# A fused chunked-attention and feed-forward kernel: how block 0's rows are loaded, and where block 2's turns stand

## The chip, the cores and the metric

The kernel runs on 1 core of one Trainium2 chip. The metric is the device time of one execution in microseconds (us), here the median of several runs. The engines are PE (TensorE; PEld are its weight loads), DVE (VectorE), ACT (ScalarE), POOL (GpSimd) and SP (SyncE). DMAs are issued from the queues of SP, ACT and Pool.

## The reference

Attention over q, k, v of shape (4 batches, 8 heads, 768 positions, 64), in chunks of 32 positions. A chunk sees 16 positions before it, itself, 8 after it, and 8 memory rows of its head (mem_k, mem_v):

```
for c in range(24):
    q_c  = q[:, :, 32*c : 32*c+32]
    ctx  = slice(max(0, 32*c-16), min(768, 32*c+40))
    k_full, v_full = concat(mem_k, k[ctx]), concat(mem_v, v[ctx])
    a = softmax(q_c @ k_full.T / 8)
    out[:, :, chunk c] = a @ v_full
x = out with heads side by side, (3072 tokens, 512)
y = (relu(x @ w_gate) * (x @ w_val)) @ w_out      # 512 -> 1536 -> 512
```

Inputs and the result are float32; the kernel computes in float16 with float32 sums in PSUM.

## The kernel before

The 3072 tokens are cut into 8 blocks of 384 (two per batch). A block's attention works on pairs of heads (hp 0 to 3). Its feed-forward part has twelve **units** of 128 hidden columns, `ffn_unit` (four g_ps matmuls, whatever stands in `between`, four v_ps matmuls, then a relu on ACT and a product gv on DVE, L323 to L351), and three output units `out_unit` (L353) with twelve o_ps matmuls each. The attention of block n + 1 is laid between the units of block n. The order of all instructions is written out by hand (`manual_schedule`), and each engine works its own list in order.

**Layout of queries and keys.** The matmuls need them turned, with the 64 dimensions on partitions. For blocks 0 to 2 the rows come in as they lie in memory (four positions a row: `k_rows`, `q_rows`, and two rows of memory keys by `load_rows_mem`) into the float16 tiles `rk` and `rq`; `turn_pe` (L177) turns them by 16 matmuls for a head pair against a selection matrix and an identity, and `turn_copy` (L196) copies the result from PSUM to SBUF on DVE, one copy for block 0 and two for blocks 1 and 2. Block 2's turn takes the PSUM tile that scores use as well (tag "sc", one buffer). From block 3 on the DMA engines turn (`turn_dma`) and Pool spreads the queries (`spread_q`).

**Block 0's rows.** A DMA from Pool's queue casts float32 to float16 on its way. SP's and ACT's don't: they bring float32 into the staging tiles `kst` and `qst`, and a copy on DVE or ACT casts it into `rk` and `rq` (`cast`, L445). Before the change heads 0 to 3 go by staging (the loop of L384: SP brings keys, ACT queries, two heads a DMA), heads 4 to 7 by Pool (L436 to L438). Pool's list then has the values of block 0 (`load_band`, four DMAs), the memory keys for the later blocks (`fetch_mem(memk, mem_k)`, L441), and the weights `load_w` in pieces of 256 columns, two DMAs each (L442, L443, L497, L498, L514, L515), with block 1's and block 2's rows and values between them. SP spreads the memory values over the value tile (`load_mem_v`, four small DMAs).

**Block 0's attention** (L461 to L508): `step_s0` (mask and score matmuls, exponential on ACT), `wide_d` (sums by matmul, then logarithm on ACT), `wide_e` (reciprocal by an exponential on ACT), `wide_v` (values by matmul, then the product xT on DVE), for each head pair. `fill` issues matmuls on a zero tile at the start. The first feed-forward matmuls of block 0 are in `chunk` (L456).

**Blocks 2 to 7** (`run`, L585): the units are gone through in order; `at` gives for each head pair the unit after which its scores are computed. Values (`step_v`) come two units later inside a unit, the product (`step_m`) three units later. For block 2, at = (2, 5, 8, 11), and a pair's turn stands one unit before its scores, behind that unit. `clear` holds six sets of DVE memsets, one behind each of the units 0 to 5.

Of the kernel before, what the change touches and what calls it, by code (L numbers as in the profile page):

```python
# [8 lines left out]
F32 = mybir.dt.float32  # L9
# [8 lines left out]
def kernel(  # L18
# [58 lines left out]

    ident = const.tile([128, 128], F16, name="ident")
    sels = [const.tile([128, NQ, 32], F16, name=f"sel{p}") for p in range(2)]
    kst = const.tile([KR + 2, H // 2, J * D], F32, name="kst")  # L80
    qst = const.tile([QR, H // 2, J * D], F32, name="qst")
    k16s = [const.tile([128, NQ, H, D], F16, name=f"k16{p}") for p in range(2)]

    vwins = [const.tile([128, NQ, H, 2 * D], F16, name=f"vwin{p}") for p in range(2)]
# [29 lines left out]
    def rows_of(n):  # L114
        if n not in rows:
            rows[n] = (half.tile([KR + 2, H, J * D], F16, tag="rk", name="rk"),
                       half.tile([QR, H, J * D], F16, tag="q16", name="rq"))
        return rows[n]

    def load_rows_mem(dma, dst, n, h0, nh):  # L120
        src = bass.AP(tensor=mem_k.tensor, offset=mem_k[n // 2, h0, 0, 0].offset,
                      ap=[[J * D, 2], [NMEM * D, nh], [1, J * D]])
        dma(dst, src)

    def load_rows(n, h0, nh):
        rk, rq = rows_of(n)
        pool_dma(rk[0:KR, h0:h0 + nh], k_rows(n, h0, nh))
        pool_dma(rq[:, h0:h0 + nh], q_rows(n, h0, nh))
# [9 lines left out]
    def fetch_mem(dst, src_t):  # L138
        pool_dma(dst, bass.AP(tensor=src_t.tensor, offset=src_t[0, 0, 0, 0].offset,
                              ap=[[D, NMEM], [NMEM * D, B * H], [1, D]]))  # L140
# [36 lines left out]
    def turn_pe(n, hp):  # L177

        if n != 1:
            pool, tag = (pools["t"], "t") if n == 0 else (sps, "sc")  # L180
            ps = pool.tile([128, 2, 512], F32, tag=tag, name="kq_ps")
            kps, qps = ps[:, 0], ps[:, 1, 0:TB]
        else:
            ps, kps, qps = None, bank("k_ps"), bank("q_ps")[:, 0:TB]
        turns[n, hp] = ps, kps, qps
        rk, rq = (t.rearrange("p h (j d) -> p h j d", j=J) for t in rows_of(n))
        sel = sels[n % 2].rearrange("p i t -> p (i t)")

        for t, dst, w in ((rk, kps, sel[0:KR + 2]), (rq, qps, ident[:QR, :QR])):
            steps = dst.rearrange("p (r j) -> p j r", j=J) if n == 0 else dst.rearrange("p (j r) -> p j r", j=J)  # L190
            for j in range(J):
                for hh in range(2):
                    nc.tensor.matmul(steps[D * hh:D * hh + D, j], lhsT=t[:, 2 * hp + hh, j], rhs=w,
                                     start=True, stop=True)

    def turn_copy(n, hp):  # L196
        if n not in kTs:
            kq = turned.tile([128, HP, 512 + TB], F16, tag="kq", name="kq")
            kTs[n] = kq[:, :, 0:512].rearrange("p a (i m) -> p i a m", i=NQ)
            qTs[n] = kq[:, :, 512:].rearrange("p a (i m) -> p i a m", i=NQ)  # L200
            turns[n] = kq
        ps, kps, qps = turns.pop((n, hp))
        if n == 0:
            dve_copy(turns[n][:, hp], ps.rearrange("p a c -> p (a c)")[:, 0:512 + TB])
        else:
            for src, dst in ((kps, turns[n][:, hp, 0:512]), (qps, turns[n][:, hp, 512:])):
                dve_copy(dst.rearrange("p (r j) -> p r j", j=J), src.rearrange("p (j r) -> p r j", j=J))  # L207
# [28 lines left out]
    def step_s0(n, hp):  # L236

        sc = sps.tile([128, 2, 512], F32, tag="sc", name="sc_ps")
        mq = bass.AP(tensor=maskq.tensor, offset=maskq.offset, ap=[maskq.ap[0], [0, NQ], [1, QB]])
        for hh in range(2):  # L240
            nc.tensor.matmul(sc[:, hh, 0:TB].rearrange("p (i m) -> p i m", m=QB), lhsT=maskk, rhs=mq,
                             start=True, stop=False)
        score_mms(n, hp, sc, False)
        ex = epool.tile([128, 2, NQ, QB], F16, tag="ex", name="ex")
        nc.scalar.activation(ex.rearrange("p h i m -> p h (i m)"), sc[:, :, 0:TB], ACT.Exp, scale=SCALE)
        exs[n, hp] = ex
# [25 lines left out]
    def wide_d(n, hp):  # L272
        ex = exs[n, hp]
        for i0, i1, kind in ((0, 1, 1), (1, NQ, 0)) if n == 0 else ((0, NQ - 1, 0), (NQ - 1, NQ, 2)):
            for hh in range(2):
                nc.tensor.matmul(xs[D * hh:D * hh + D, QB * i0:QB * i1], lhsT=ones[:, kind, :],
                                 rhs=ex[:, hh, i0:i1, :], start=True, stop=True)
        nc.scalar.activation(xs, xs, ACT.Ln, scale=1.0 / 64.0)

    def wide_e(n, hp):  # L280
        rinv = rpool.tile([128, TB], F32, tag="rw", bufs=4, name="rw")
        nc.scalar.activation(rinv, xs, ACT.Exp, scale=-1.0, bias=mln64)
        rinvs[n, hp] = rinv

    def wide_v(n, hp):
        ex = exs.pop((n, hp))
        for i in range(NQ):
            for hh in range(2):
                nc.tensor.matmul(xo[D * hh:D * hh + D, QB * i:QB * i + QB], lhsT=vwins[n][:, i, 2 * hp + hh, 0:D],
                                 rhs=ex[:, hh, i, :], start=True, stop=True)  # L290
        nc.vector.tensor_tensor(out=x_of(n)[:, hp, :], in0=xo, in1=rinvs.pop((n, hp)), op=ALU.mult)
# [87 lines left out]
    def fill(count):  # L379
        for i in range(count):  # L380
            nc.tensor.matmul(xo, lhsT=filler[:, 0:128], rhs=filler[:, 0:TB], start=True, stop=True)


    for hp in range(HP // 2):  # L384
        sp(kst[0:KR, 2 * hp:2 * hp + 2], k_rows(0, 2 * hp, 2))
        act_dma(qst[:, 2 * hp:2 * hp + 2], q_rows(0, 2 * hp, 2))
        if hp == 0:
            load_rows_mem(sp, kst[KR:KR + 2], 0, 0, H // 2)
    nc.scalar.preload_act_table_set("natural_log_exp_and_others")

    def words(t):
# [41 lines left out]
    select(ident, 1.0, 0, [[-1, 128]], 1)  # L433
    build_sel(0)
    fetch_mem(memv, mem_v)
    load_rows(0, 4, 2)  # L436
    load_rows_mem(pool_dma, rows_of(0)[0][KR:KR + 2, H // 2:H], 0, H // 2, H // 2)
    load_rows(0, 6, 2)  # L438
    load_band(0, v, vwins)
    load_mem_v(0)  # L440
    fetch_mem(memk, mem_k)  # L441
    load_w(0, 256)  # L442
    load_w(256, 512)  # L443

    def cast(t, hp, eng):  # L445
        dst, src, n = rows_of(0)[t], (kst, qst)[t], (KR + 2, QR)[t]
        eng(dst[0:n, 2 * hp:2 * hp + 2], src[:, 2 * hp:2 * hp + 2])
# [11 lines left out]
                ffn_mm(n, x, f, a)  # L459

    with tc.tile_pool(name="tps", bufs=2, space=bass.MemoryType.PSUM) as pools["t"]:  # L461
        fill(12)
        cast(0, 0, dve_copy)
        for t, hp in ((1, 0), (1, 1), (0, 1)):
            cast(t, hp, act_copy)
        turn_pe(0, 0)
        turn_copy(0, 0)
        fill(4)
        step_s0(0, 0)
        turn_pe(0, 1)  # L470
        turn_copy(0, 1)
        wide_d(0, 0)
        wide_e(0, 0)
        step_s0(0, 1)
        turn_pe(0, 2)
        turn_copy(0, 2)
        wide_d(0, 1)
        wide_e(0, 1)
        turn_pe(0, 3)
        turn_copy(0, 3)  # L480
    pools["f"] = ctx.enter_context(tc.tile_pool(name="fps", bufs=4, space=bass.MemoryType.PSUM))
    step_s0(0, 2)
    wide_v(0, 0)
    wide_d(0, 2)
    step_s0(0, 3)
    wide_e(0, 2)


# [6 lines left out]
    select(bias, 0.0, -NMEM, [[0, 3]], 1, ALU.is_ge)  # L495
    select(bias, NEG, NMEM + 55, [[32, 3]], -1, ALU.is_ge)
    load_w(512, 768)  # L497
    load_w(768, 1024)  # L498

    ffn_open(0, (0, 1))  # L500
# [78 lines left out]
    def pieces(n, what):  # L579
        for w, hp in what:  # L580
            STEP[w](n, hp)
# [3 lines left out]
    def run(order, n, at, turn_at):  # L585
        for u, (b, x) in enumerate(order):
            now = [hp for hp in range(HP) if n < NB and u == at[hp] + 2]
            if n < NB:
                pieces(n, [("m", hp) for hp in range(HP) if u == at[hp] + 3])
            inner, outer = ("ve", "") if x >= NDC else ("v", "e")  # L590
            unit(b, x, [lambda w=(w, hp): pieces(n, [w]) for hp in now for w in inner])
            pieces(n, [(w, hp) for hp in now for w in outer])
            if n < NB:
                pieces(n, [("s", hp) for hp in range(HP) if u == at[hp]])
            if n == 2:
                for hp in range(HP):
                    if u == at[hp] - 1:
                        turn_pe(n, hp)
                        turn_copy(n, hp)
                if u < len(clear):  # L600
                    clear[u]()
            if u == turn_at and n + 1 < NB:
                turn_dma(n + 1)
                spread_q(n + 1)
# [44 lines left out]
```

## Time and profile before

| what | value |
|---|---|
| median of 7 runs | 241.52 us (240.37 to 242.7) |
| the profiled execution | 240.37 us, span 238.5 us |
| PE busy | 227.0 us, 95% of the span |
| ACT busy | 142.2 us, 60% |
| DVE busy | 105.5 us, 44% |
| POOL busy | 101.5 us, 43% |
| packets of Pool's queue (q0), share of 16 engines over the span | 80.4% |
| packets of SP's (q1) and ACT's queue (q10) | 19.9%, 8.5% |

A share of busy time is a mean over stages that have different limits, so it has to be read by stretches of time. Columns named "idle before" give the time that an engine stood still before an instruction, and after "<-" what ended it. Packets overlap in the DMA engines, so their summed share can be over 100%. The bytes of a casting DMA are counted as they are written, at half of what is read.

### The profile page before, as it was taken

Reading aid. Unit: us, or ns where it says so; the run is one execution under the profiler, and the core shown is the slowest. Engines: PE = TensorE matmul, PEld = TensorE weight load, DVE = VectorE, ACT = ScalarE, POOL = GpSimd, SP = SyncE. Lnnn points to the kernel's source line nnn. Section 1 sums busy time; section 2 is a strip of 40 time slices with the busy share of each in tenths; the row PEclk is TensorE's granted clock in tenths of the full one; section 3 lists DMA queues with packets and bytes.
Section 4 is the critical chain, followed back from the end, with each engine's and each line's share of the span. In section 5 each row is a group of like instructions: output and inputs, shape, how many; then the busy total and the mean of one; then the engine's idle time right before and its main releaser. Section 6 shows DMA issues by size and latency. Waiting matters only on the chain.

```text
span 238.5 us, 4610 instructions
## 1 busy us (share of the span) xinstructions
PE 227.0 (95%) x1736; PEld 131.0 (55%) x1736; DVE 105.5 (44%) x208; ACT 142.2 (60%) x300; POOL 101.5 (43%) x129
## 2 busy tenths in 40 slices
PE   7869799999999999999999999999999999999993
PEld 3635454555544566546664666556664666456541
DVE  3545647878611055612662146505551266313400
ACT  3663494377752388827984489628892698434321
POOL 8998665935219901990069503980130000000000
PEclk9999999999999999999999999999999999999998
DMA  7999999999997999599929997999902100120012
GB/s 164 137 165 194 193 179 195 174 192 148 127 160 119 193 168 132 35 166 129 175 28 111 195 143 80 65 186 138 137 0 83 49 3 0 47 88 0 1 44 88
DMA packets 107831, 27.61 MB, mean 116 GB/s; under 512 B 91730, under 2 KB 104866, under 8 KB 107810
## 3 DMA queue, kind: packets, MB, share of 16 engines
q0 software_dynamic: 82560, 15.16, 80.4%
q1 hardware_dynamic: 21378, 5.61, 19.9%
q10 hardware_dynamic: 3872, 6.56, 8.5%
q8 instruction: 13, 0.21, 0.3%
q14 instruction: 8, 0.07, 0.1%
HBM read 31.13 MB, written 6.29 MB: 157 GB/s over the span
## 4 chain that ended last, share of the span: by engine, by line
PE 75%; DMA 12%; POOL 5%; DVE 4%; ACT 2%; issue 2%; POOLq 0%; DVEq 0%
PE o_ps L360 25%; PE g_ps L334 22%; PE v_ps L334 21%; DMA wv<-in_moe_w_val_dram 11%; PE sc_ps L258 3%; DVE kq L207 2%; PE xo_ps L298 2%; PE xs_ps L298 2%; POOL vwin L136 2%; DVE gv L341 1%; DMA out_dram<-o_sb 1%; ACT ln L302 1%; POOL wg L166 1%; ACT gr L340 1%; PE sc_ps L233 1%
## 5 line engine op out<-in xcount | busy, mean ns | idle before, releaser
L341 DVE TENSOR_TENSOR gv<-v_ps,gr 128x384 f16<-128x384 f32 x95 | 52.8, 557 | 98.9 <-ACT gr L340 85.7
L334 PE MATMUL v_ps<-xT,wv 128*128 128x384 f16 x380 | 78.3, 326 | 1.1 <-DMA wv<-in_moe_w_val_dram 1.0
L334 PE MATMUL g_ps<-xT,wg 128*128 128x384 f16 x380 | 78.4, 326 | 0.0
L360 PE MATMUL o_ps<-wo,gv 128*128 128x512 f16 x288 | 63.5, 379 | 0.0
L340 ACT ACTIVATE gr<-g_ps 128x384 f16<-128x384 f32 x95 | 46.1, 486 | 19.7 <-PE g_ps L334 9.6
L334 PEld LDWEIGHTS <-wv 128*128 128x128 f16 x384 | 36.0, 98 | 23.9 <-DMA wv<-in_moe_w_val_dram 2.5
L334 PEld LDWEIGHTS <-wg 128*128 128x128 f16 x384 | 36.0, 98 | 22.3
L360 PEld LDWEIGHTS <-gv 128*128 128x128 f16 x288 | 28.1, 98 | 32.9
L221 POOL COPY qbd<-qT 64x1536 f16<-64x1536 f16 x10 | 14.6, 1462 | 58.5 <-DMA qT<-q16n 58.2
L264 ACT ACTIVATE ex<-sc_ps,bias 128x256 f16<-128x256 f32 x84 | 33.3, 467 | 8.2 <-PE sc_ps L233 7.6
L369 ACT COPY o_sb<-o_ps 128x512 f32<-128x512 f32 x23 | 13.5, 585 | 39.2 <-PE o_ps L360 31.2
L136 POOL DMA_DIRECT2D vwin<-in_v_dram x32 | 29.0, 932 | 3.7 <-DMA rk<-in_mem_k_dram 1.5
L307 ACT ACTIVATE rinv<-ln,mln 64x768 f32<-64x768 f32 x24 | 22.2, 923 | 0.0
L302 ACT ACTIVATE ln<-xo_ps 64x384 f32<-64x384 f32 x24 | 11.7, 487 | 14.8 <-PE xs_ps L298 14.8
L162 POOL DMA_DIRECT2D q16n<-in_q_dram x20 | 15.6, 802 | 5.7 <-DMA wo<-in_moe_w_out_dram 5.7
L136 POOL DMA_DIRECT2D k<-in_k_dram x20 | 17.9, 907 | 0.2 <-issue 0.2
L313 DVE TENSOR_TENSOR xT<-xo_ps,rinv 64x384 f16<-64x384 f32 x24 | 13.1, 546 | 10.2 <-ACT rinv L307 10.2
L313 DVE TENSOR_TENSOR xT<-xs_ps,rinv 64x384 f16<-64x384 f32 x24 | 13.2, 551 | 0.7
L298 PEld LDWEIGHTS <-vwin 128*128 128x128 f16 x192 | 10.8, 98 | 3.2
L302 ACT ACTIVATE ln<-xs_ps 64x384 f32<-64x384 f32 x24 | 11.4, 475 | 0.0
L298 PE MATMUL xo_ps<-ex,vwin 128*128 128x96 f16 x96 | 11.1, 206 | 0.0
L298 PE MATMUL xs_ps<-ex,vwin 128*128 128x96 f16 x96 | 11.1, 206 | 0.0
(73 smaller groups left out, 132.3 us busy)
## 6 DMA issues: line engine op xcount, KB each, us to landing
out_dram<-o_sb ACTq DMA_DIRECT2D x23, 256.0 KB
vwin<-in_v_dram POOLq DMA_DIRECT2D x24, 120.0 KB, 9.2
q16n<-in_q_dram POOLq DMA_DIRECT2D x20, 96.0 KB, 5.1
k<-in_k_dram POOLq DMA_DIRECT2D x15, 120.0 KB, 4.4
wg<-in_moe_w_gate_dram POOLq DMA_DIRECT2D x6, 256.0 KB, 7.9
wv<-in_moe_w_val_dram POOLq DMA_DIRECT2D x6, 256.0 KB, 8.5
wo<-in_moe_w_out_dram POOLq DMA_DIRECT2D x3, 512.0 KB, 10.2
rk<-in_k_dram POOLq DMA_DIRECT2D x4, 224.0 KB, 8.0
```

Of the source, the lines that this page charges most:

```text
L136: pool_dma(dsts[p][NMEM + m0:NMEM + m1, i, :, 0:D], src)
L162: pool_dma(q16s[n][:, i], src)
L221: nc.gpsimd.tensor_copy(qbds[n % 2][s, :, :, hh, :].rearrange("p i a m -> p (i a) m"), qTs[n][s].rearrange("p i a m -> p (i a) m"))
L264: nc.scalar.activation(flat[:, :, :, s], view[:, :, :, s], ACT.Exp, scale=SCALE, bias=bias[:, g:g + 1])
L298: nc.tensor.matmul((xo, xs)[hh][:, QB * i:QB * i + QB], lhsT=vw[:, i, 2 * hp + hh, :], rhs=ex[:, hh, i, :], start=True, stop=True)
L302: nc.scalar.activation(ln[:, hh], (xo, xs)[hh][D:128], ACT.Ln, scale=1.0 / 64.0)
L307: nc.scalar.activation(rinv, lns.pop((n, hp)), ACT.Exp, scale=-1.0, bias=mln64[0:D, :])
L313: nc.vector.tensor_tensor(out=x_of(n)[D * hh:D * hh + D, hp, :], in0=(xo, xs)[hh][0:D], in1=rinv[:, hh, :], op=ALU.mult)
L334: nc.tensor.matmul(ps[a], lhsT=(wg, wv)[a][:, f, 128 * m:128 * m + 128], rhs=xTs[n][:, f, :], start=(f == 0), stop=(f == NFC - 1))
L340: nc.scalar.activation(gr, g_ps, ACT.Relu)
L341: nc.vector.tensor_tensor(out=gvs[n][:, m, :], in0=v_ps, in1=gr, op=ALU.mult)
L360: nc.tensor.matmul(o_ps, lhsT=gvs[n][:, m, 128 * t:128 * t + 128], rhs=wo[:, m, :], start=(m == 0), stop=(m == NDC - 1))
```

## The change

Heads 4 and 5 of block 0 go by staging and casting too, so that heads 0 to 5 come by SP's and ACT's queues and only heads 6 and 7 by Pool's. The casts of all queries are on ACT, those of all keys on DVE, the second cast ahead of the first turn's copy and the third ahead of the second's. In the first stretch two turns stand on PE ahead of the first scores, with fewer fillers, and the later steps are ordered anew. The memory keys' fetch moves on Pool's queue from ahead of all weights to between two later pieces of them. Block 2's turns move from behind a unit to between its g_ps and v_ps matmuls.

```diff
@@ -77,8 +77,8 @@
 
     ident = const.tile([128, 128], F16, name="ident")
     sels = [const.tile([128, NQ, 32], F16, name=f"sel{p}") for p in range(2)]
-    kst = const.tile([KR + 2, H // 2, J * D], F32, name="kst")
-    qst = const.tile([QR, H // 2, J * D], F32, name="qst")
+    kst = const.tile([KR + 2, H - 2, J * D], F32, name="kst")
+    qst = const.tile([QR, H - 2, J * D], F32, name="qst")
     k16s = [const.tile([128, NQ, H, D], F16, name=f"k16{p}") for p in range(2)]
 
     vwins = [const.tile([128, NQ, H, 2 * D], F16, name=f"vwin{p}") for p in range(2)]
@@ -381,11 +381,11 @@
             nc.tensor.matmul(xo, lhsT=filler[:, 0:128], rhs=filler[:, 0:TB], start=True, stop=True)
 
 
-    for hp in range(HP // 2):
+    for hp in range(HP - 1):
         sp(kst[0:KR, 2 * hp:2 * hp + 2], k_rows(0, 2 * hp, 2))
         act_dma(qst[:, 2 * hp:2 * hp + 2], q_rows(0, 2 * hp, 2))
         if hp == 0:
-            load_rows_mem(sp, kst[KR:KR + 2], 0, 0, H // 2)
+            load_rows_mem(sp, kst[KR:KR + 2], 0, 0, H - 2)
     nc.scalar.preload_act_table_set("natural_log_exp_and_others")
 
     def words(t):
@@ -433,12 +433,10 @@
     select(ident, 1.0, 0, [[-1, 128]], 1)
     build_sel(0)
     fetch_mem(memv, mem_v)
-    load_rows(0, 4, 2)
-    load_rows_mem(pool_dma, rows_of(0)[0][KR:KR + 2, H // 2:H], 0, H // 2, H // 2)
-    load_rows(0, 6, 2)
+    load_rows(0, H - 2, 2)
+    load_rows_mem(pool_dma, rows_of(0)[0][KR:KR + 2, H - 2:H], 0, H - 2, 2)
     load_band(0, v, vwins)
     load_mem_v(0)
-    fetch_mem(memk, mem_k)
     load_w(0, 256)
     load_w(256, 512)
 
@@ -459,30 +457,32 @@
                 ffn_mm(n, x, f, a)
 
     with tc.tile_pool(name="tps", bufs=2, space=bass.MemoryType.PSUM) as pools["t"]:
-        fill(12)
+        fill(11)
+        for hp in range(HP - 1):
+            cast(1, hp, act_copy)
         cast(0, 0, dve_copy)
-        for t, hp in ((1, 0), (1, 1), (0, 1)):
-            cast(t, hp, act_copy)
+        cast(0, 1, dve_copy)
         turn_pe(0, 0)
         turn_copy(0, 0)
-        fill(4)
+        turn_pe(0, 1)
+        cast(0, 2, dve_copy)
+        turn_copy(0, 1)
+        fill(1)
         step_s0(0, 0)
-        turn_pe(0, 1)
-        turn_copy(0, 1)
+        turn_pe(0, 2)
+        turn_copy(0, 2)
         wide_d(0, 0)
         wide_e(0, 0)
         step_s0(0, 1)
-        turn_pe(0, 2)
-        turn_copy(0, 2)
-        wide_d(0, 1)
-        wide_e(0, 1)
         turn_pe(0, 3)
         turn_copy(0, 3)
     pools["f"] = ctx.enter_context(tc.tile_pool(name="fps", bufs=4, space=bass.MemoryType.PSUM))
+    wide_d(0, 1)
     step_s0(0, 2)
+    wide_e(0, 1)
     wide_v(0, 0)
+    step_s0(0, 3)
     wide_d(0, 2)
-    step_s0(0, 3)
     wide_e(0, 2)
 
 
@@ -495,6 +495,7 @@
     select(bias, 0.0, -NMEM, [[0, 3]], 1, ALU.is_ge)
     select(bias, NEG, NMEM + 55, [[32, 3]], -1, ALU.is_ge)
     load_w(512, 768)
+    fetch_mem(memk, mem_k)
     load_w(768, 1024)
 
     ffn_open(0, (0, 1))
@@ -588,17 +589,14 @@
             if n < NB:
                 pieces(n, [("m", hp) for hp in range(HP) if u == at[hp] + 3])
             inner, outer = ("ve", "") if x >= NDC else ("v", "e")
-            unit(b, x, [lambda w=(w, hp): pieces(n, [w]) for hp in now for w in inner])
+            turning = [hp for hp in range(HP) if n == 2 and u == at[hp] - 1]
+            unit(b, x, [lambda hp=hp: (turn_pe(n, hp), turn_copy(n, hp)) for hp in turning]
+                 + [lambda w=(w, hp): pieces(n, [w]) for hp in now for w in inner])
             pieces(n, [(w, hp) for hp in now for w in outer])
             if n < NB:
                 pieces(n, [("s", hp) for hp in range(HP) if u == at[hp]])
-            if n == 2:
-                for hp in range(HP):
-                    if u == at[hp] - 1:
-                        turn_pe(n, hp)
-                        turn_copy(n, hp)
-                if u < len(clear):
-                    clear[u]()
+            if n == 2 and u < len(clear):
+                clear[u]()
             if u == turn_at and n + 1 < NB:
                 turn_dma(n + 1)
                 spread_q(n + 1)
```

## The prediction

> **What bounds the kernel now.** I read the busy time by stage first, then the chain of waits, then the timeline of the stages that are not full. The stages, with columns from:to, length, busy time (instructions) of PE, PEld, DVE, ACT and POOL, granted clock, DMA share and GB/s:
>
> ```profile
> 0.00:16.68 16.68, 12.87 (x152) 7.54 (x153) 7.71 (x26) 9.43 (x14) 15.99 (x32) 1.00 1.30 153
> 16.68:40.00 23.32, 21.35 (x240) 11.66 (x238) 12.90 (x26) 14.13 (x33) 15.82 (x23) 1.00 1.59 190
> 40.00:65.18 25.18, 23.15 (x237) 13.63 (x236) 20.04 (x40) 14.65 (x32) 14.34 (x17) 1.00 1.73 163
> 65.18:232.20 167.02, 167.02 (x1102) 97.17 (x1102) 64.43 (x117) 102.99 (x220) 55.40 (x58) 1.00 0.94 96
> ```
>
> From 65.18 to 232.2 PE is never idle, so nothing can be won or lost there unless an input comes late. The change acts on three stretches before: the start (until the first feed-forward matmul at 16.68), the stretch in which weights still land (to 40), and block 2's turns (to 65.18). The chain of waits says what limits the second: the landing of weights on Pool's queue, the last of them at 30.40 + 9.38 = 39.78. The timeline of PE shows the places (start, length, count, idle before it and who ended it):
>
> ```profile
> 30.40 9.38 DMA wv<-in_moe_w_val_dram
> ...
> 25.91 0.82 PE L334 MATMUL g_ps<-xT,wg 128*128 128x384 f16 x4
> 27.61 0.82 PE L334 MATMUL v_ps<-xT,wv 128*128 128x384 f16 x4 [0.88 <-DMA wv<-in_moe_w_val_dram]
> ...
> 35.17 0.82 PE L334 MATMUL g_ps<-xT,wg 128*128 128x384 f16 x4
> 36.04 0.82 PE L334 MATMUL v_ps<-xT,wv 128*128 128x384 f16 x4
> ...
> 38.95 0.82 PE L334 MATMUL g_ps<-xT,wg 128*128 128x384 f16 x4
> ```
>
> Four such matmuls take 0.65 from start to start (28.93 to 29.59 less switching), so the waits for weights are 27.61 - 25.91 - 0.65 = 1.05, 36.04 - 35.17 - 0.65 = 0.22 and 39.83 - 38.95 - 0.65 = 0.23; with 0.33 at the first v_ps (17.17, when 16.68 + 0.16 was possible) 1.83 us in all. PE without them would need 39.83 - 16.68 - 1.83 = 21.3 us from the first feed-forward matmul to the last weights.
>
> The third stretch:
>
> ```profile
> 46.06 0.81 PE L334 MATMUL v_ps<-xT,wv 128*128 128x384 f16 x4
> 47.37 0.34 PE L233 MATMUL sc_ps<-kq 64*128 64x96 f16 x8 [0.50 <-DVE kq L207]
> ...
> 44.93 0.91 DVE L451 MEMSET vwin<- 128x1024 uint32 x1 [0.16 <-issue]
> 45.76 0.49 DVE L341 TENSOR_TENSOR gv<-v_ps,gr 128x384 f16<-128x384 f32 x1
> 46.17 1.14 DVE L207 CAST kq<-kq_ps 128x512 f16<-128x512 f32 x2
> ```
>
> The scores stand behind the turn's two copies on DVE: 47.37 - (46.06 + 0.65) = 0.66 us of PE. The chain has the same at 53.19, 59.02 and 64.84, every 5.82 us.
>
> **What the Trainium skill says.** "DMA: Bandwidth & Descriptors", section "SWDGE vs HWDGE vs iDMA", says that only GpSimd's DMAs can cast; the trace agrees in that the staged rows (kst, qst) need casts on DVE (0.43 us) and ACT (0.62). The same page, "Issuing engines are not separate DMA queues", says that all issuers' DMAs interleave on the same 16 engines and that spreading them saves only issue time. The trace partly differs here: at 3 to 4 us, with SP's and ACT's queues alone, 350 GB/s are written; from 4 to 6 us it is 253 and 184, and Pool's first packet starts only at 4.75 though its first DMA was issued at 1.85. So there is unused capacity which the hardware queues could fill. "TensorE: Matmul & The Clock Gate", Part 1, says that the array runs at half rate until about 3.4 us of activity, and again after as long an idle window; the fillers agree (0.32 us apart from 1.26 on, 0.16 from 5.94 on).
>
> **The change, part by part.**
>
> *Start, staging.* SP and ACT issue one DMA more each (0.32 and 0.47, before their first waits: hidden by ACT's wait for qst until 4.79). Heads 4 and 5 (224 + 192 KB in f32) leave Pool's queue. Before, the second kst landed at 6.93 (ACT's cast began then). The third qst now shares the engines with it; I take 7.2 (6.9 if SP's queue isn't slowed, 7.8 if it gets half of what it had), and the third kst at 8.6 (224 KB at about 180 KB/us beside Pool's traffic, and the 1.3 us that passed between the last packet of SP's queue, 5.64, and the landing).
>
> *Start, order on DVE.* This is the edit with a price: cast k1 now stands ahead of copy 0, and cast k2 ahead of copy 1, on an engine that works in order. Cast k1 7.25 to 7.68 (0.43), copy 0 to 8.81 (1.09; before 7.14). First exponential, 0.38 after its scores: 9.23 to 10.04 (before 7.58). Cast k2 to 9.28, turn 2 on PE to 10.2; then sums, logarithm, reciprocal (0.39 + 0.47 + 0.6) to 11.7; second exponential 11.72 to 12.53 (before 10.13). Third: 0.28 of sums, 0.45 of mask and 0.38 more, so 13.68 to 14.49 (before 12.87); fourth 0.87 later, 15.36 to 16.17 (before 15.06, where 0.8 us had been lost to the memory rows of the values, 13.91 on PE; these now come behind a shorter queue and are covered). Logarithm and reciprocal of pair 2, now behind the fourth exponential: 17.28. Last sums 17.33, first feed-forward matmul **17.6, 0.9 later** than 16.68. Four fillers fewer cost nothing: PE waits there anyway, and its hole, some 5.95 to 7.7, stays shorter than the idle window named above; if the array did slow down, each four-matmul group until it recovers would cost 0.65 more.
>
> *Pool's queue.* Pool issues two row loads (0.67 + 0.62) and memk (0.67) less ahead of the weights; its memory-row load stays, halved. What counts is the queue behind: PE waits for landings, not for issues. 112 + 96 + 4 = 212 KB leave it; at the 194 GB/s of 20 to 21 us that is 1.1 us. Against this stand 416 KB more on the hardware queues: 1.2 us at 350 GB/s if all of it displaces Pool's packets, nothing if it fills the gap at 4 to 6 us. So every later landing moves by between +0.1 and -1.1; most of the gap is free, I take -0.8. Memk (32 KB in small packets, some 0.3 us) only changes its place: it helps the first six weight loads, not the last six; its reader is SP's load at 22.25, whose result is needed by the transposes at 59.
>
> *To 40 us.* By PE: 17.6 + 21.3 = 38.9. By landing: 39.78 - 0.8 = 39.0. The last weights are used at about 39.05 instead of 39.83: **0.8 us won** (ends: -0.6 with the first feed-forward matmul at 19.1, +1.1 with full shift and 17.4).
>
> *Block 2's turns.* PE's work between scores is 0.28 (scores) + 3 x 1.30 (units) + 0.52 (turn) + 0.34 (values) = 5.04. The turn moves 0.65 ahead (half a unit), and its copies get ahead of that unit's gv (0.57) on DVE. The score bank is free in time: the three exponentials end 1.59 after the scores start (47.37 to 48.96), the next turn comes 2.23 after. But DVE is nearly full until the six clears (units 0 to 5) are done, so I follow it, in the times of before. Copies 0 start behind the clear at 45.77 and end 46.91; scores 46.97 (before 47.37). Then gv, clear, gv, clear, gv, clear (0.57, 0.76, 0.57, 0.76, 0.55, 0.9 with their gaps) to 51.0, copies 1 to 52.1; scores 52.15, where PE could at 52.01 (before 53.19). Then gv, clear, two xT products (1.1), gv, clear, gv to 56.35, copies 2 to 57.47; scores 57.52, where PE could at 57.19 (before 59.02). After that no clears: DVE is done before PE, scores at 57.52 + 5.04 = 62.56 (before 64.84). **2.3 us won**, of 4 x 0.66 = 2.64 at most; at least 1.0, if DVE keeps a period of 5.6.
>
> *What is late next.* wo, and block 3's keys and queries. Pool's spread of block 3 ends at 73.7; its scores come 1.3 after 81.0, so at 79.2 when all is 3.1 earlier: 5 us to spare. After 65.18 nothing else changes.
>
> **Sum.** The profiled execution took 240.37 (span 238.5 and 1.9 around it), the lowest of the seven; the median of 241.52 is 1.15 higher. 240.37 - 0.8 - 2.3 = 237.3; on the median **238.4**.
>
> **Rivals.** (1) *The start eats its gain*: the kst landings come 0.5 us later than I took, or the added hardware traffic displaces Pool's, so that the stretch to 40 gives 0 or loses half a microsecond, and DVE holds the turns. For it: casts stand ahead of copies. Against it: unused DMA capacity. Gain 1.2 to 2.3: 239.2 to 240.3. (2) *All of it comes*: landings 1.1 earlier, first feed-forward matmul by 17.2, copies never wait: 1.1 + 2.64 = 3.7 or a little more: 237.2 to 237.8. Against it: DVE's share at 40 to 65 is 20.04 of 25.18. (3) *Slower: the third kst lands late.* Everything on DVE stands behind cast k2. Up to a landing at 9.3 ACT covers it, beyond that the first feed-forward matmul is 17.6 + (landing - 9.3). The gain of the turns is used up when PE reaches the last weights at 39.83 + 2.3, so with a start at 20.8, a landing at 12.5. At 14.5: 42.1 + 2.0, so 243.5. For it: Pool's queue fills all engines from 6 us on. Against it: the hardware queues wrote 832 KB by 5.64, and 224 KB would need 7 us more. (4) *No change*: the turns give 1.0 and the start loses 0.6 or more: within 0.5%.
>
> **How the numbers follow.** Half a per cent, 1.2 us, is about what a measurement of this kernel tells from no change. My forecast (gain 2.4 to 3.6) 0.54; (1) 0.21; (2) 0.12; no change 0.08; slower 0.05. Faster 0.54 + 0.21 + 0.12 = 0.87. The range takes in (1) and (2): 237.2 to 240.3, which leaves out 0.13 and the edges.
>
> **What would show it.** Right: second kst cast on DVE near 7.2 and copy 0 behind it; first feed-forward matmul 17.2 to 18; no wait for weights over 0.3 us after it; last weights landing near 39; scores of block 2 about 5.2 to 5.6 us apart, the last interval 5.04; first o_ps near 62. Wrong: a score still waiting 0.5 us or more for kq each time; a first feed-forward matmul after 19; last weights landing at 39.8; a new wait after o_ps begins.

## The result, and the profile after

| | before | after |
|---|---|---|
| median of all runs | 240.52 us (26 runs, 239.81 to 242.7) | 241.74 us (11 runs, 240.75 to 243.6) |
| the profiled execution, its span | 240.37, 238.5 | 241.07, 239.3 |
| mean granted TensorE clock in it | 0.997 | 0.984 |

The ratio of after to before is 1.0056, 95% interval 1.0031 to 1.008: the change costs 1.2 us where 2.4 to 3.6 were forecast as gain. (The median of before is 1 us lower with more runs than the one the prediction started from; the ratio is measured side by side and does not depend on that.) Ratios leave out executions that took over 1.5% longer than the fastest of their kernel; medians take in all of them.

The stages of after, cut at the same three events as those of before: the first feed-forward matmul, the first use of the last weights, the first o_ps matmul after block 2's turns. Columns as in the prediction: from:to, length, busy time (count) of PE, PEld, DVE, ACT and POOL, granted clock, DMA share, GB/s. After:

```profile
0.00:20.20 20.20, 15.36 (x149) 9.18 (x149) 8.97 (x28) 9.14 (x14) 17.49 (x36) 0.91 1.40 180
20.20:42.95 22.75, 21.90 (x239) 12.14 (x238) 12.51 (x25) 13.94 (x32) 17.72 (x23) 0.93 1.67 185
42.95:66.08 23.13, 23.10 (x238) 13.66 (x236) 19.98 (x40) 14.17 (x32) 9.78 (x12) 1.00 1.80 173
66.08:233.00 166.92, 166.92 (x1105) 97.11 (x1101) 64.92 (x117) 103.27 (x222) 55.31 (x58) 1.00 0.90 93
```

and before, where the second and third stage are cut at 39.83 and 65.11:

```profile
16.68:39.83 23.15, 21.18 (x239) 11.55 (x237) 12.73 (x25) 13.96 (x33) 15.82 (x23) 1.00 1.60 190
39.83:65.11 25.28, 23.25 (x236) 13.66 (x236) 20.14 (x41) 14.82 (x32) 14.34 (x17) 1.00 1.73 163
```

The third stage shrank by 2.15 us (25.28 to 23.13). The last is the same. The whole loss is ahead of 42.95: the last weights are used 3.12 us later than before (39.83), and 3.12 - 2.15 = 0.97 is left at the first o_ps. Two columns give the place: the first stage is 3.5 us longer with no more instructions on PE (149 for 152), and the clock column, 1.00 throughout before, reads 0.91 and 0.93. (This column, and the mean clocks below, count only from the first clock record on. The time until then, in which the array is not yet at full rate, stands in them as 1.00.)

PE's timeline of after in the first stage (start, length, instruction, in brackets the idle time before it and what ended it):

```profile
1.26 3.70 PE L381 MATMUL xo_ps<-filler 128*128 128x384 f16 x11 [1.26 <-DVE filler L394]
5.78 1.06 PE L193 MATMUL kq_ps<-sel,rk 114*64 114x128 f16 x8 [0.81 <-DVE rk L445]
...
14.86 0.23 PE L289 MATMUL xo_ps<-ex,vwin 128*64 128x96 f16 x2 [0.25 <-DMA vwin<-memv]
15.96 0.23 PE L289 MATMUL xo_ps<-ex,vwin 128*64 128x96 f16 x2 [0.88 <-DMA vwin<-memv]
16.42 0.23 PE L289 MATMUL xo_ps<-ex,vwin 128*64 128x96 f16 x2 [0.22 <-DMA vwin<-memv]
...
19.74 0.53 PE L276 MATMUL xs_ps<-ex,ones 128*64 128x96 f16 x4 [1.12 <-ACT rw L282]
20.20 0.50 PE L334 MATMUL g_ps<-xT,wg 128*128 128x384 f16 x1
```

The same places before:

```profile
13.91 0.23 PE L289 MATMUL xo_ps<-ex,vwin 128*64 128x96 f16 x2 [0.78 <-DMA vwin<-memv]
...
16.68 0.34 PE L334 MATMUL g_ps<-xT,wg 128*128 128x384 f16 x1
```

After the change, the first value matmuls wait three times for `vwin<-memv`, SP's small spreads of the memory values, 1.35 us in all (0.78 before). They stand on PE ahead of the last pair's mask and scores, which therefore start only at 16.58, and the fourth exponential is at 17.88 (before 15.06). The chain of waits after (start, length, piece; SPq is SP's queue) says the same from the other side:

```profile
10.57 0.69 SPq L152
11.29 4.99 DMA vwin<-memv
...
16.65 0.75 PE sc_ps L241 x2
17.88 0.81 ACT ex L245
```

SP could issue these spreads only once Pool's `memv` had landed, at 8.83; before, at 7.07. Pool issued it at 1.8 in both. The first packet of Pool's queue starts at 6.24 instead of 4.75, when SP's and ACT's queues, now one DMA longer each, are nearly empty (last packets at 7.37 and 7.08; before 5.64 and 4.76). GB/s of after between 4 and 6 us, when only those two queues move data for the kernel:

```profile
4.00:5.00 1.00, 0.96 (x4) 0.15 (x1) 0.16 (x1) 0.00 (x0) 1.00 (x2) 1.00 1.13 244
5.00:6.00 1.00, 0.23 (x4) 0.23 (x6) 0.72 (x1) 0.93 (x2) 1.00 (x2) 1.00 1.10 253
```

Next the clock. In the clock records of after, the array has full rate from 9.75 (before: from 4.82), half rate from 16.58 to 23.40, and full rate from there to the last 0.9 us. In all 14 traces of this study, every stretch between two changes of the rate is a whole multiple of 3.413 us long (after: 6.827, 6.827 and 215.04). So I count windows of 3.41 us from the first record of full rate. Of after:

```profile
13.16:16.58 3.42, 1.86 (x22) 0.98 (x22) 1.07 (x1) 1.92 (x4) 3.31 (x7) 1.00 1.49 191
16.58:19.99 3.41, 2.29 (x28) 1.28 (x26) 1.11 (x2) 1.77 (x3) 2.33 (x4) 0.50 1.52 195
19.99:23.40 3.41, 3.41 (x19) 1.21 (x16) 0.56 (x1) 1.06 (x2) 3.16 (x5) 0.50 1.45 196
```

and the two least busy of before, counted in the same way:

```profile
11.65:15.06 3.41, 2.63 (x48) 1.46 (x44) 2.11 (x3) 2.08 (x4) 3.41 (x8) 1.00 1.49 148
15.06:18.48 3.42, 2.18 (x27) 1.12 (x26) 0.80 (x2) 2.34 (x4) 3.19 (x8) 1.00 1.45 185
```

The window with the waits has PE busy for 1.86 us, and the next two run at half rate. No single idle stretch in it is longer than 0.9 us. The feed-forward matmuls from 20.20 to 23.4 follow one another at 0.32 us instead of 0.16.

Block 2's turns, on PE after:

```profile
54.51 0.81 PE L334 MATMUL v_ps<-xT,wv 128*128 128x384 f16 x4
55.26 0.34 PE L233 MATMUL sc_ps<-kq 64*128 64x96 f16 x8
...
60.55 0.34 PE L233 MATMUL sc_ps<-kq 64*128 64x96 f16 x8
```

The bracket with `DVE kq` that stood behind the scores before is gone; they are 5.25 to 5.29 us apart (before 5.82).

### The profile page after: what moved, and what is told of

Its sections match the earlier page's. It is cut to its first block, busy times and chain, and to the rows that moved or that the text cites. A ratio compares the mean times of both kernels' runs of the same rounds, so it can differ in the third digit from the quotient of the medians.

```text
span 239.3 us, 4604 instructions
## 1 busy us (share of the span) xinstructions
PE 230.0 (96%) x1732; PEld 133.2 (56%) x1732; DVE 106.8 (45%) x210; ACT 141.5 (59%) x300; POOL 100.3 (42%) x127
## 4 chain that ended last, share of the span: by engine, by line
PE 88%; DMA 5%; DVE 3%; ACT 2%; SPq 1%; issue 1%; DVEq 0%
PE g_ps L334 26%; PE v_ps L334 26%; PE o_ps L360 25%; PE sc_ps L258 3%; DMA vwin<-memv 2%; PE xo_ps L298 2%; PE xs_ps L298 2%; DMA kst<-in_k_dram 2%; PE kq_ps L193 2%; PE sc_ps L233 1%; SPq L152 1%; PE xo_ps L289 1%; DVE kq L207 1%; DMA out_dram<-o_sb 1%; PE gv_ps L334 1%
## 5 line engine op out<-in xcount | busy, mean ns | idle before, releaser
L334 PEld LDWEIGHTS <-wg 128*128 128x128 f16 x384 | 36.5, 98 | 23.0 <-issue 0.6
```

The costliest lines, as they stand in the source:

```text
L334: nc.tensor.matmul(ps[a], lhsT=(wg, wv)[a][:, f, 128 * m:128 * m + 128], rhs=xTs[n][:, f, :], start=(f == 0), stop=(f == NFC - 1))
```

## The experiments

The theory at this point: the turns bring what they were to bring; the start loses more, through late memory rows of the values and the halved clock that follows. Rivals: the casts on DVE or their late third landing (the prediction's own way to a loss); and that the order of Pool's queue, not its late beginning, sets the loss. Medians of before in the four groups of runs: 240.64, 240.77, 240.62 and 240.58. Each kernel below shares its group with a run of before; ratios are to that.

| kernel | median us | range | ratio to before (95%) | first feed-forward matmul |
|---|---|---|---|---|
| e1_turns_only | 238.21 | 237.76 to 238.58 | 0.9874 (0.9829 to 0.9918) | 16.82 |
| e2_start_only | 243.79 | 243.13 to 245.03 | 1.0113 (1.0067 to 1.016) | 20.18 |
| e3_fillers_in_hole | 241.36 | 238.92 to 243.03 | 0.9993 (0.9967 to 1.002) | 19.47 |
| e4_values_later | 238.72 | 238.08 to 239.98 | 0.9897 (0.9852 to 0.9941) | 18.66 |
| e5_mem_by_sp | 240.61 | 237.6 to 241.91 | 0.9962 (0.9937 to 0.9986) | 20.68 |
| e6_turns_memk | 238.49 | 237.47 to 239.64 | 0.9898 (0.9863 to 0.9934) | 17.32 |
| e7_mem_late | 241.86 | 240.44 to 243.13 | 1.0042 (1.0023 to 1.0061) | 19.17 |
| e8_one_pair | 239.59 | one run | | 17.74 |
| e9_later_and_warm | 239.77 | 237.27 to 241.45 | 0.9943 (0.9921 to 0.9964) | 18.96 |
| e10_turns_values_later | 238.42 | 238.18 to 240.17 | 0.9928 (0.9904 to 0.9952) | 17.60 |
| e11_later_all_filled | 239.35 | 239.0 to 240.04 | 0.9951 (0.9935 to 0.9967) | 20.61 |
| e12_changed_all_filled | 239.09 | 238.93 to 239.31 | 0.9939 (0.9925 to 0.9952) | 19.64 |

### The two halves of the change apart

e1 is the kernel before with the last hunk of the change alone; e2 is the changed kernel without that hunk.

```diff
-            unit(b, x, [lambda w=(w, hp): pieces(n, [w]) for hp in now for w in inner])
+            turning = [hp for hp in range(HP) if n == 2 and u == at[hp] - 1]
+            unit(b, x, [lambda hp=hp: (turn_pe(n, hp), turn_copy(n, hp)) for hp in turning]
+                 + [lambda w=(w, hp): pieces(n, [w]) for hp in now for w in inner])
```

> The kernel before with block 2's turns inside the units and nothing else. Theory (the loss is all in the start, the turns pay as forecast): scores of block 2 at 5.0 to 5.3 us from each other instead of 5.82, some 2.1 us faster than before, so about 238.4. Rival (the turns lose, DVE's copies come in the way of the unit's own product): 240 or more.

> The changed kernel with block 2's turns behind the units again: staging, casts, Pool's order and the order of block 0's steps alone. Theory: first feed-forward matmul near 20 again and the whole start loses 3.1 us against before, so about 243.7. Rival (start and turns are not independent, the late start is made up in the turns' slack): 242 or less.

Measured: e1 238.21, that is 2.43 us faster than before; e2 243.79, 3.15 slower. The halves add up within what can be told: -2.43 + 3.15 = +0.72, where the change measured +1.22. In e1 the array keeps full rate from 4.69 to the end. PE's timeline of e1:

```profile
27.84 0.82 PE L334 MATMUL v_ps<-xT,wv 128*128 128x384 f16 x4 [1.25 <-DMA wv<-in_moe_w_val_dram]
...
51.29 0.81 PE L334 MATMUL v_ps<-xT,wv 128*128 128x384 f16 x4
52.04 0.34 PE L233 MATMUL sc_ps<-kq 64*128 64x96 f16 x8
```

The scores follow their unit without a wait, as in after. The wait for weights at 27.84 is the one that a later start hides: in after no matmul waits for weights. So a start that is up to some 1.8 us late (the sum of these waits before, an estimate) should be paid back here.

### Fillers in the hole, and the values later

Here a hole is a stretch in which PE stands idle. There are two ways to take the clock's fall away. e3 keeps PE busy where it waits; e4 lets the last scores pass the waiting value matmuls.

```diff
     wide_e(0, 1)
+    fill(12)
     wide_v(0, 0)
```

```diff
     wide_e(0, 1)
-    wide_v(0, 0)
     step_s0(0, 3)
     wide_d(0, 2)
     wide_e(0, 2)
+    wide_v(0, 0)
```

> The changed kernel with 12 fillers ahead of the first value matmuls of block 0, so that PE has work while the memory rows of the values land (about 2 us). Theory (the wait costs twice, as a wait and by the halved clock from 16.6 to 23.4 us that follows it): no stretch at half clock after 10 us, first feed-forward matmul near 19, the whole some 2 to 2.7 us faster than the changed kernel, so about 239.4. Rival 1 (the clock is a side show, only the landing counts): within 0.6 us of the changed kernel. Rival 2 (the casts' order on DVE sets the start): no change either.

> The changed kernel with the first value matmuls of block 0 behind the scores of pair 3 and the sums of pair 2, so that these don't stand behind the wait for the memory rows. Theory (PE works in order and the wait for the memory rows holds up the last scores): fourth exponential near 15.6 instead of 17.9, first feed-forward matmul near 18, 2 to 3.5 us faster than the changed kernel, 238.3 to 239.8, the more if the clock stays up. Rival 2 (the casts' order on DVE sets the start): first feed-forward matmul stays after 19.5, time within 0.6 us.

e4 is 3.0 us below the changed kernel (241.74 - 238.72), with the fourth exponential at 16.52 (17.88 in after, expected 15.6) and its profiled execution's clock at 0.998. ACT's timeline of e4:

```profile
16.52 0.81 ACT L245 ACTIVATE ex<-sc_ps 128x768 f16<-128x768 f32 x1 [0.38 <-PE sc_ps L233]
```

The casts and their order are those of the changed kernel, so they are not behind these 3.0 us: the last scores' place behind the waiting value matmuls is. (What is left of the late start, 18.66 against e1's 16.82, has still the late full rate in it, from 10.19.) e3's median, 241.36, lies where its first rival put it, within 0.6 us of the changed kernel. But its executions spread by the mean clock granted to each: 238.9 to 239.1 at 1.0, most of those at 0.986 from 241.6 to 242.4. In one and the same kernel the fall of the clock thus goes with 2.5 us and more. The profiled execution is of the first kind. Its least busy window at the start holds the next hole (the wait ahead of the last sums):

```profile
16.94:20.35 3.41, 1.97 (x35) 1.20 (x36) 0.86 (x2) 2.52 (x5) 2.87 (x4) 1.00 1.51 196
```

So one hole was filled. That this second one decided the other executions is likely but not shown, as only the profiled one has a trace.

### Why the memory rows are late

Four kernels ask whether the late `memv` is enough for the loss, and what makes it late. e5 lets SP fetch block 0's memory values in float32 by itself, between its first and second kst; DVE casts them.

```diff
             load_rows_mem(sp, kst[KR:KR + 2], 0, 0, H - 2)
+            sp(mv32, bass.AP(tensor=mem_v.tensor, offset=mem_v[0, 0, 0, 0].offset,
+                             ap=[[D, NMEM], [NMEM * D, H], [1, D]]))
...
-    load_mem_v(0)
...
         cast(0, 0, dve_copy)
+        dve_copy(mv16, mv32)
+        load_mem_v(0)
         cast(0, 1, dve_copy)
```

> The changed kernel, but block 0's memory rows of the values come by SP's queue in float32 behind the first staged keys, are cast on DVE, and SP spreads them from there; they no longer wait for Pool's queue to start. Theory (the late memory rows are the whole of the loss): no wait for them in the first value matmuls, no stretch at half clock, first feed-forward matmul at 17.6 to 18.2, weights never waited for, so 237.5 to 238.3. Rival (six staged pairs and their casts delay the start by themselves): first feed-forward matmul at 19 or later, 239.5 or more.

By the numbers set ahead, the rival came true (first feed-forward matmul at 20.68, 240.61 us). But e5 does not separate the two: the memory rows are no longer waited for, and yet something new came in. The second cast waited for its keys and began at 7.76 instead of 6.50; the small DMA that now stands ahead of them on SP's queue is the likely reason. PE's timeline of e5:

```profile
8.70 1.06 PE L195 MATMUL kq_ps<-sel,rk 114*64 114x128 f16 x8 [1.22 <-DVE rk L448]
```

The array had full rate only from 13.41. (This profiled execution took 241.57, near the upper end of its range; the best took 237.6.)

e7 makes the rows late without staging anything more, in e1; e6 does the memory keys' part of the change alone, in e1 too:

```diff
-    fetch_mem(memv, mem_v)
     load_rows(0, 4, 2)
...
     load_rows(0, 6, 2)
+    fetch_mem(memv, mem_v)
```

```diff
     load_mem_v(0)
-    fetch_mem(memk, mem_k)
     load_w(0, 256)
...
     load_w(512, 768)
+    fetch_mem(memk, mem_k)
```

> The kernel before with block 2's turns inside the units, and the memory values' fetch moved on Pool's queue behind the rows of heads 4 to 7, so that they land late while everything else of the start stays as before. Theory (late memory rows make the hole and the halved clock, without any of the six-head staging): first value matmuls wait until 15 or later, first feed-forward matmul 1 to 2 us later than 16.8, in most executions a stretch of half clock behind it, so 239.3 to 241. Rival (they are covered, the loss comes from staging and casts): within 0.5 us of 238.2.

> The kernel before with block 2's turns inside the units and, of the changed start, only the memory keys' fetch moved behind the third piece of weights; four heads staged as before. Theory: the first six weight loads land 0.2 to 0.4 earlier, the wait for the third piece (1.3 us in the kernel with the turns alone) is shorter by that, so 237.8 to 238.1. Rival (later landings count alone, which don't move): 238.2 as with the turns alone.

e7 is the clearest run of the study. With four heads staged as before, and `memv` landing at 8.57, it takes 241.86: 3.65 us more than e1, more than was expected, and no less than the start of the changed kernel costs (3.15, e2). PE's timeline of e7, and its windows of 3.41 us:

```profile
15.08 0.23 PE L289 MATMUL xo_ps<-ex,vwin 128*64 128x96 f16 x2 [1.01 <-DMA vwin<-memv]
16.23 0.23 PE L289 MATMUL xo_ps<-ex,vwin 128*64 128x96 f16 x2 [0.92 <-DMA vwin<-memv]
...
19.17 0.50 PE L334 MATMUL g_ps<-xT,wg 128*128 128x384 f16 x1
```

```profile
14.12:17.53 3.41, 1.54 (x26) 0.93 (x27) 0.72 (x2) 1.23 (x3) 3.03 (x6) 1.00 1.46 189
17.53:20.95 3.42, 2.34 (x22) 0.96 (x15) 0.56 (x1) 2.18 (x4) 2.16 (x6) 0.50 1.50 196
```

The waits are longer than in after (1.93 us for 1.35), the first feed-forward matmul comes 2.35 us later than in e1, and the clock falls in the same way, 1 us later than in after. So late rows alone are enough for a loss of this size, without a further staged head. e6 takes 238.49 against e1's 238.21: the first six weight loads land up to 0.45 us earlier (27.43 for 27.80), the last six about 0.4 later, and no gain can be told from that.

e8 asks what holds Pool's queue at the start: e1 with one pair staged instead of two.

```diff
-    for hp in range(HP // 2):
+    for hp in range(1):
         sp(kst[0:KR, 2 * hp:2 * hp + 2], k_rows(0, 2 * hp, 2))
         act_dma(qst[:, 2 * hp:2 * hp + 2], q_rows(0, 2 * hp, 2))
         if hp == 0:
-            load_rows_mem(sp, kst[KR:KR + 2], 0, 0, H // 2)
+            load_rows_mem(sp, kst[KR:KR + 2, 0:2], 0, 0, 2)
...
     fetch_mem(memv, mem_v)
+    load_rows(0, 2, 2)
     load_rows(0, 4, 2)
-    load_rows_mem(pool_dma, rows_of(0)[0][KR:KR + 2, H // 2:H], 0, H // 2, H // 2)
+    load_rows_mem(pool_dma, rows_of(0)[0][KR:KR + 2, 2:H], 0, 2, H - 2)
...
-        for t, hp in ((1, 0), (1, 1), (0, 1)):
+        for t, hp in ((1, 0),):
```

> The kernel before with block 2's turns inside the units, with only heads 0 and 1 staged and heads 2 to 7 by Pool. A look at when Pool's queue starts. Theory (Pool's packets hardly move while the two hardware queues are full: first packets at 4.7 with two pairs staged, near 6 with three): first packet at 3.4 to 3.8, memory values landed at 5.5 to 6. Rival (Pool's own setting up takes until 4.7): first packet at 4.6 to 4.8 and memory values at about 7, as with two pairs.

The tile `memv` of e8:

```profile
DMA to landing us min/median/max: 3.4/3.4/3.4
```

and in after it reads 7.0, in before 5.2, for the same 32 KB issued at 1.8. Pool's first packet starts at 3.72, 4.75 and 6.24 with one, two and three pairs staged. Had Pool's own preparation set its beginning, e8 would have shown 4.7 again. The rows' fetch is the first on Pool's queue in all three, so the order of that queue is not what makes them late in after.

### Values later without the staging, and a warm array

e9 is e4 with three fillers more at the start; e10 is e1 with the value matmuls moved as in e4.

```diff
-        fill(11)
+        fill(14)
```

> The changed kernel with the first value matmuls behind the scores of pair 3 (as in e4_values_later) and 14 fillers at the start instead of 11, so that PE works until the first turn at 5.8. Theory (the second hole, 5.0 to 5.8, keeps the array at half clock until 9 to 10 us, where the kernel before has it up at 4.8): clock up by 7, first exponential near 9.3 instead of 10.7, first feed-forward matmul near 17.8, 237.7 to 238.2. Rival (what is left of the late start is the keys' landing and the casts, not the clock): within 0.3 us of 238.7.

> The kernel before with block 2's turns inside the units and the first value matmuls behind the sums of pair 2 and the scores of pair 3, four heads staged. Theory (there the memory rows land in time but for 0.2 us, so the order there hardly matters): 237.9 to 238.3, no difference that can be told from the turns alone. Rival (the wait for memory rows costs there too): 237.6 or less.

e10 is e1 within what can be told (238.42 and 238.21): where the rows come in time, passing the value matmuls gains nothing. e9, at 239.77, missed its range and its rival's. It got what it asked for at the start (full rate from 4.46, first exponential at 9.52) and lost it later: everything came sooner to the same late memory rows, PE was busy for 1.47 us of the window from 14.70 to 18.11, and the clock was halved from 18.11 to 21.53. At a clock of 1.0 its three executions take 237.3 to 238.5, at 0.986 seven take 240.2 to 241.5. The start of the full rate goes with the fillers over all kernels: 4.46 to 5.54 in the three with 14 at the beginning, 6.70 to 13.41 in the five with 11, and 4.69 to 7.29 in those of before's start with 12 and four more.

### All holes filled

e12 is the changed kernel with fillers in every hole of the start: 14 for 11 at the beginning, 4 between the first two turns, 12 ahead of the first values, 8 ahead of the last sums. e11 does the same to e4, with 8 ahead of the first values.

```diff
         turn_copy(0, 0)
+        fill(4)
         turn_pe(0, 1)
...
+    fill(12)
     wide_v(0, 0)
...
     wide_v(0, 1)
+    fill_bank(8)
     wide_d(0, 3)
```

> The changed kernel in its own order, with 14 fillers at the start, 4 between the first two turns, 12 ahead of the first value matmuls and 8 ahead of the last sums; the memory rows land as late as in the changed kernel. Theory (of the late start's price most is clock, the wait itself costs under 1 us): mean granted clock 0.998 or more, 238.3 to 239. Rival (the wait is the price): 240.5 or more at full clock.

> The kernel of e9_later_and_warm with fillers in the three holes that are left on PE: 4 between the first two turns, 8 ahead of the first value matmuls, 8 (in a bank of their own) ahead of the last sums. Theory (the time goes with the number of 3.4 us windows at half clock in the start, and a window is lost when PE stands idle for a good part of it): mean granted clock 0.998 or more in nearly all executions, 237.3 to 237.8 with a spread under 1 us. Rival (the clock falls for another reason than PE's own holes): levels at 0.99 and 0.986 as before, median 239 or more.

e12 met its expectation but for 0.1 us: five executions within 0.4 us of each other, all at a clock of 1.0. Its windows of 3.41 us:

```profile
11.95:15.36 3.41, 3.13 (x31) 1.57 (x26) 1.09 (x1) 2.16 (x4) 3.41 (x9) 1.00 1.52 197
15.36:18.78 3.42, 2.87 (x37) 1.72 (x37) 1.11 (x2) 1.26 (x3) 2.68 (x6) 1.00 1.54 197
```

The memory rows come as late as in after (its value matmuls still wait for them at 16.51), so 241.74 - 239.09 = 2.65 us is what the half rate costs in the changed kernel, late warm-up and fall together, if the fillers themselves cost nothing; where they do, it is more. e3's executions at a clock of 1.0 come to the same time (238.9 to 239.1).

e11 kept its clock (0.997 to 1.0) and missed its time, 237.3 to 237.8. PE's timeline of e11 tells why:

```profile
18.91 1.47 PE L387 MATMUL fl_ps<-filler 128*128 128x384 f16 x8
20.32 0.36 PE L276 MATMUL xs_ps<-ex,ones 128*64 128x96 f16 x4
20.61 0.34 PE L334 MATMUL g_ps<-xT,wg 128*128 128x384 f16 x1
```

There is no hole to fill any more: what the sums need was ready at 17.1, and eight fillers stand in their way for 1.4 us.

## Why the prediction was wrong, step by step

- **Block 2's turns: right, in mechanism and size.** Forecast -2.3 us; -2.15 in the profile of after, -2.43 between the medians of e1 and before. PE's own period is 5.25 us, not 5.04, and no copy is waited for.
- **The casts on DVE: right in time, wrong as the danger.** The second cast began at 6.50 (7.2 forecast) and the third waited for nothing at 8.56. The way forecast to a slower kernel, a late third kst, did not occur. The first exponential came at 10.28, not 9.23, though copy 0 ended at 8.61, even ahead of the forecast (8.81): PE worked without a pause from 5.78, but the two turns ahead of the scores ran at half rate (a group of eight took 1.06 for 0.63). With a warm array, e12 has it at 9.31.
- **"these now come behind a shorter queue and are covered": the step that failed.** The shorter queue was Pool's. But the fetch of the memory values is the first on it, ahead of the rows that left, so nothing became shorter for it; and Pool's queue did not begin until the longer hardware queues had nearly ended. The memory rows landed at 8.83 instead of 7.07, the waits for them grew from 0.78 to 1.35 us, and the last pair's scores stood behind them. The first feed-forward matmul came at 20.20, not 17.6. e4, which lets the scores pass, wins 3.0 us back; e7 shows that late rows alone are enough for such a loss, and e8 that the staged pairs set when they come. The reading behind this step was the unused capacity: 350 GB/s at 3 to 4 us were taken as what the hardware queues could have kept up. In after they had the engines to themselves until 6.24, and wrote 244 and 253 at 4 to 6 us. At 245, the added 416 KB take 1.7 us (an estimate), about what the memory rows came later.
- **The hole on PE that "stays shorter than the idle window named above": the second one.** True of each hole, and of no use. The prediction took from the Trainium skill, "TensorE: Matmul & The Clock Gate", Part 1, a length of idling; in these traces holes far shorter than that went with half rate (the last section). The four fillers fewer that were to "cost nothing" left a hole from 4.96 to 5.78, and the array came to full rate at 9.75 instead of 4.82; the later holes halved it again from 16.58. The text did price the halved rate at 0.65 a group, and then left it out of the sum.
- **Pool's queue: direction right, and worth nothing.** The last weights landed at 37.73 in after, 2.05 earlier than before (0.8 forecast, 1.1 at most; over the kernels with its staging 37.4 to 38.5, against 38.8 to 39.8 with four staged heads, so about 1.3 between the means). But PE came to them at 42.95. The stretch to their use was taken as limited by landings and became limited by PE: 3.52 us later at its beginning, less 1.83 of waits for weights that went away, leaves 1.43 by which PE's part ran longer. The half rate up to 23.4 accounts for it (3.2 us at half rate lose 1.6, an estimate).
- **The memory keys' place: right**, nothing to be seen (e6).

The loss can be divided by medians: turns -2.43 (e1 against before), half rate +2.65 (after against e12), the rest of the late start net of the waits it hides +0.88 (e12 against e1). These three add up to after less before by construction, so the sum proves nothing. The independent check is that of the two halves, e1 and e2.

What six staged heads could bring with the rows in time and a warm array is not shown. e4, which still has the late warm-up, is 0.5 us above e1, and their ranges overlap.

The best kernel of the study by its median is e1_turns_only, the turns alone, at 238.21: 0.9874 of before, and 3.5 us below the changed kernel. e10, e6 and e4 lie about 0.5 us or less above it.

Still open: why Pool's queue hardly moves while the hardware queues are full (only that it starts late with them is shown); why the first cast of the keys took 0.43 us in some kernels and up to 0.88 in others; and what SP's fetch of the memory rows would bring without the delay that e5 brought along (its fastest execution, 237.60, is below all of e1's).

## What to carry to other kernels

When a transfer moves to a faster queue, look for what stays on the slow one and is needed soon, the transfers at its head above all: a queue that begins later delays its first small transfer too, and on an engine that works in order one waiting matmul holds up everything behind it. Where PE has holes, add up its busy time over windows of the clock's length instead of looking only for the longest gap, and price a halved clock into the sum rather than beside it. Before paying for an earlier start, see whether the following stage waits for its data anyway: here about 1.8 us of lateness at the start could hide in the waits for weights, and what came beyond that could not (e12 starts 2.8 us later than e1 and costs 0.9).

## What the runs showed of the hardware

**The longest gap does not tell whether the clock falls; the busy time of a window tells it better.** Every stretch between two changes of the rate is a multiple of 3.413 us in the 14 profiled executions: 6.83, 10.24 or 13.65 at full rate before a fall, 3.41 or 6.83 at half rate. Counted back from the first record of full rate, the edges of these windows lie anywhere from 0.4 to 3.4 us after the first instruction, so they don't follow the kernel. At the start the rate was halved after six windows, in which PE's records were busy for 1.36 to 1.93 us (after 1.86, e2 1.93, e5 1.36, e7 1.54, e9 1.47, e10 1.91), and after no window at full rate with 1.97 (e3) or more. The longest gap orders these windows wrongly:

```profile
16.80 0.23 PE L289 MATMUL xo_ps<-ex,vwin 128*64 128x96 f16 x2 [0.56 <-DMA vwin<-memv]
```

is the longest in e2's window, which was followed by half rate, and

```profile
19.18 0.36 PE L276 MATMUL xs_ps<-ex,ones 128*64 128x96 f16 x4 [1.44 <-ACT rw L282]
```

is in e3's, which kept the rate. But the busy time is not the whole rule either. At the end of the execution, where PE runs out of work, the windows with at most 1.27 us were followed by half rate, and two with 1.64 (e3) and 1.72 (e8) by full rate, although 1.86 to 1.93 were too little at the start. The ends of matmuls are modelled, and no run varied the busy time by itself, so from these traces the edge lies somewhere between 1.5 and 2.0 us of 3.41, and no closer. To come back, a window at half rate needed more: those with 2.29 to 2.34 us (after, e2, e7) were followed by another at half rate, those with 3.35 or more by full rate.

The windows also decide whether a hole does harm: before, the stretch from 13.40 to 16.68 had only 1.68 us of work, but an edge at 15.06 cut it in two, and the rate was kept. The Trainium skill has the like, "TensorE: Matmul & The Clock Gate", section "A second HAM failure mode: psum-queue depth-cycling", where frequent short idling makes the clock swing; these traces agree, with no hole over 0.9 us in the window of after. That the edges fall differently from one execution to the next would explain why e3 and e9 spread over 4 us and e12, without such holes, over 0.4; their mean clocks agree, but only the profiled executions show the edges.

**Pool's queue began later with every pair staged on the hardware queues.** 32 KB issued first on Pool's queue at 1.8 landed at 5.26 with one staged pair (e8), 6.98 to 7.13 with two (four kernels), and 8.68 to 9.00 with three (eight kernels): about 1.8 us for each pair of 416 KB, nearly as if those had to end first. "DMA: Bandwidth & Descriptors", section "Queues, rings and completion order", of the Trainium skill says that each DMA engine goes round robin over the queues that have work, a packet at a time. By that Pool's packets should have come in between from the start; in after the first came at 6.24, about 1 us before the hardware queues' last. The trace shows packets only when they move, so whether Pool's queue had any ready in that time stays open; e8 shows only that they can start at 3.72.
